# The first three q, k units of an attention kernel, made together by chunks of tokens

## The chip, the cores and the metric

The kernel runs on one core of one Trainium2 chip, in one launch. The metric is the device time of the kernel in microseconds, the median of the runs shown. The core has five engines with a queue of instructions each: TensorE (PE, with its weight loads shown apart as PEld), VectorE (DVE), ScalarE (ACT), GpSimd (POOL) and SyncE (SP, which here only issues DMAs). Engines wait for each other and for DMAs through semaphores.

## The reference

The layer is a sum of two branches on the same tokens, mixed by a gate of each token:

```python
x = A_x                                              # 1 x 2048 x 448
g = _sigmoid((x * gate_w).sum(-1, keepdims=True))
qkv = (x @ wqkv).reshape(B, S, 3, H, Dh)             # 16 heads of 28
p = softmax(q k^T * Dh ** -0.5);  a = (p v) @ wo
gate = x @ W_gate; gate = gate * (gate > 0)          # 448 x 1792
b = (gate * (x @ W_up)) @ W_down
return g * a + (1 - g) * b
```

All arrays are float32. The tokens are the same `x` in both branches.

## The kernel before, in words

Float32 operands are split into a high part (rounded to the format in which TensorE multiplies fast) and a low part, the remainder. `act_high` (line 130, ACT) makes the high part; `low` (line 136, DVE) or `pool_low` (line 139, POOL) subtracts it from the source. A product then has three terms: high by high, low by high, high by low. The 448 input features lie as four chunks of 128 partitions (the last is 64 features twice), so one output tile is the sum of the eleven matmuls of `TERMS`: a pair (a, b) takes part a of the weights `W` and part b of the tokens, and b % 4 is the chunk.

The first 100 us or so make q, k and v. Tokens come in four blocks of 512 (`tb`), weights in groups of 224 columns, which is 4 heads of k and q halves (`GD` = 112, two of it). A **unit** (tb, c), function `qk`, is 128 columns of q, k for one block of tokens: 11 matmuls (line 352) into one PSUM bank, then ACT copies the high part out, DVE makes the remainder (both into a tile `st` or half of the unused tile `K2`), and POOL issues a DMA (line 359) that stores both to `qk_d` in DRAM. A v unit (`vproj`, line 370) makes 128 tokens of v. The banks of units go round in a ring of four (0, 1, 5, 4); three `st` tiles and two halves of `K2` go round in a ring of five, and the sixth unit made waits for the store of the first.

Head h's K and Q are then fetched back from `qk_d` by SP (lines 175, 180, 182), four row blocks each and a block of zeros, and the first score matmul (line 191) reads all of K0 and Q0. The fetch of head 0 needs the units (0,0), (1,0), (2,0), (3,0) stored.

The order of work is written out by hand: each engine runs its queue in the order in which the code calls it. The first lines of the program are `load_w`, `load_x` (DMAs), `split_first` (the first weight group and the first tokens, by chunks), `split_w`, `split_x`, and calls of `qk`. Eleven matmuls on zeros ahead of the first unit (line 398, `WARM`) keep TensorE running until data come. The three staging tiles `xr` for tokens go round (`bufs=3`), the staging tile `wr` for weights is a single one, and the space of `V[:, 1]`, not needed until later, is used as a second one. POOL also fills rows of `K0`, `K1` (line 411) and columns of `V` (lines 406, 407) before its first store.

Of the kernel before, what the change touches and what calls it, by code (L numbers as in the profile page):

```python
# [18 lines left out]
P = 128  # L19
# [5 lines left out]
GD = G * DH  # L25
# [8 lines left out]
NQ = 2 * D // P  # L34

WC = 1408
WARM = 11

EARLY = (5, 5, 4, 4, 4, 3, 3, 3, 2, 2, 2, 2, 1, 1, 1, 1)

# [38 lines left out]
def gated_mix_kernel(ctx, tc, x, wq, wo, wgu, wd, out):  # L79
# [49 lines left out]
    def act_high(dst, src):  # L129
        nc.scalar.activation(dst, src, AF.Copy)  # L130
# [90 lines left out]
    def xf(tb, b):  # L221
        return X[tb][b // 4][:, b % 4]
# [13 lines left out]
    with tc.tile_pool(name="qkv", bufs=1) as pa:  # L236
        W = pa.tile([P, 7, WC], F32R, name="W")

        def load_w(c):
            c0, c1 = c * 2 * GD, (c + 1) * 2 * GD if c < G + 1 else 2 * D + VC  # L240

            if c in (0, 2, 5):
                wr = V[:, 1].rearrange("p k h d -> p (k h d)")[:, :4 * (2 * GD + 2)]
                wr = wr.rearrange("p (c n) -> p c n", c=4)
            else:
                wr = pa.tile([P, 4, 2 * GD + 2], F32, name=f"wr_{c0}", tag="wr", bufs=1)
            wr = wr[:, :, :c1 - c0]
            if c > 0:
                nc.sync.dma_start(wr, wq[:, :, c0:c1])
            return wr, c0, c1  # L250

        def split_w(wr, c0, c1):

            ways = [[(W[:, :, c0:c1], wr)]]
            if c0 < 2 * D:
                w, r = (ap.rearrange(f"p c {n} -> p c a j d", a=2, j=4)
                        for ap, n in ((W[:, :, c0:c1], "(j a d)"), (wr, "(a j d)")))
                ways = [[(w[:, :, a], r[:, :, a]) for a in range(2)]]

                if c0 == 2 * GD:  # L260
                    ways = [[(w[:, :, :, 0], r[:, :, :, 0])], [(w[:, :, a, 1:], r[:, :, a, 1:]) for a in range(2)]]
            for way in ways:
                for w, r in way:
                    act_high(w[:, 0:3], r[:, 0:3])
                    low(w[:, 3:6], r[:, 0:3], w[:, 0:3])
                for w, r in way:
                    act_high(w[:, 6], r[:, 3])
                    low(w[64:, 6], r[64:, 3], w[64:, 6])

        def split_first(wr, xr):  # L270

            r = wr.rearrange("p c (a j d) -> p c a j d", a=2, j=4)
            w = W[:, :, :2 * GD].rearrange("p c (j a d) -> p c a j d", a=2, j=4)

            def weights(c):
                act_high(w[:, c if c < 3 else 6], r[:, c])
                yield

                take = pool_low if c else low
                if c < 3:  # L280
                    take(w[:, 3 + c], r[:, c], w[:, c])
                else:
                    take(w[64:, 6], r[64:, 3], w[64:, 6])
                yield

            def tokens(c):
                part = xr[c // 2][2][:, c % 2:c % 2 + 1]
                act_high(X[0][0][:, c:c + 1], part)
                yield
                low(X[0][1][:, c:c + 1], part, X[0][0][:, c:c + 1])  # L290
                yield

            for group in ((weights(0), tokens(0)), (weights(1), tokens(1)), (weights(2), weights(3)),
                          (tokens(2), tokens(3))):
                for _ in range(2):
                    for part in group:
                        next(part)

        def load_x(tb):
            r = []  # L300
            for c in range(0, 4, 2):
                xr = pa.tile([P, 2, TB], F32, name=f"xr_{tb}_{c}", tag="stg", bufs=3)
                for a, b in ((c, c + 1), (c + 1, c + 2)) if tb == 0 else ((c, c + 2),):
                    nc.sync.dma_start(xr[:, a - c:b - c], x[:, a:b, tb * TB:(tb + 1) * TB])  # L304
                if tb + c == 0:
                    load_first(nc.sync, 2, 4)
                r.append((c, c + 2, xr))
            return r

# [39 lines left out]
        def qk(tb, c, terms=TERMS, among=()):  # L349
            ps = ps_any(c == NQ - 1)  # L350
            for n, (a, b) in enumerate(terms):
                nc.tensor.matmul(ps, W[:, a, c * P:(c + 1) * P], xf(tb, b), start=(n == 0), stop=(n == NT - 1))  # L352
                mix(n, among)
            st = st_tile(tb, c)

            def send():
# [21 lines left out]
                    nc.gpsimd.dma_start(v_d[g][:, k - 3:k + 1], V[:, g, k - 3:k + 1])  # L378


        w0 = load_w(0)

        def load_first(queue, a, b):
            queue.dma_start(w0[0][:, a:b], wq[:, a:b, w0[1]:w0[2]])  # L384
# [24 lines left out]
        split_first(w0[0], x0)  # L409
        for k in K[:2]:  # L410
            nc.gpsimd.memset(f32(k)[96:128], -1.0)
# [24 lines left out]
        w3 = load_w(3)  # L436
        load_k(0)
        load_q(0)

# [451 lines left out]
```

## Time and profile before

| | |
|---|---|
| median of 3 runs | 1259.94 us (1259.93 to 1260.57) |
| span of the profiled execution, first to last instruction | 1258.2 us |
| the median of the runs, less that span | 1.74 us |
| PE busy | 1252.8 us, 100% |
| DVE, ACT, POOL busy | 854.8, 748.4, 374.3 us |
| q, k and v matmuls by chunks of x (line 352) | 308, in 28 units of 11 |
| DMA share, 20 to 30 us | 1.04 and 1.02 by slices of 5 us |

A line of the timeline gives start, duration, engine, line, operation, output and inputs, shape, count, and in brackets the idle time ahead of it and what ended it. A line of the chain gives start, duration and what the end of the program hung on there. In tables by stage, columns are the stretch, its length, then busy time and count of PE, PEld, DVE, ACT and POOL, the granted share of TensorE's clock, the busy share of the DMA engines and GB/s. A DMA line gives the transfer, the queue, the count, its size, and the time from issue to landing where it is known. `q0` is the queue of POOL's DMAs, `q1` that of SP's, `q10` that of ACT's. A busy PE is not PE at its peak, since the ends of matmuls are modelled.

### The profile page before, as it was taken

To read this page: it belongs to the slowest core of one execution; us is meant where nothing else is said; L and a number is where in the kernel's file an instruction comes from. 1 tells how busy PE (TensorE), PEld (TensorE's weight loads), DVE (VectorE), ACT (ScalarE), POOL (GpSimd) and SP (SyncE) were. 2 spreads that over 40 slices of the span, in tenths; PEclk is the share of its full clock that TensorE was granted. 3 is DMA by queue.
4 is the path that set the end of the run, shared out by engine and by line. 5 is a ranking of instruction groups with operands and counts; after the bars stand their busy time and mean duration, and the time that the engine had idled before them with its cause. 6 is when DMAs were issued, how large, how long until landed. Compare 5 with 4: busy or idle time off the path is not lost.

```text
span 1258.2 us, 18270 instructions
## 1 busy us (share of the span) xinstructions
PE 1252.8 (100%) x6687; PEld 919.1 (73%) x6687; DVE 854.8 (68%) x1363; ACT 748.4 (59%) x1424; POOL 374.3 (30%) x569
## 2 busy tenths in 40 slices
PE   9999999999999999999999999999999999999998
PEld 6888866677666676666766667766667666899997
DVE  6599767687777797776977778877778224663342
ACT  6312767686666776666866667766677773312121
POOL 4222222312334123423133331134222444651020
PEclk9999999999999999999999999999999999999999
DMA  8955453144245314241544323142431226634432
GB/s 302 315 206 209 117 155 99 50 106 104 60 115 173 81 43 121 68 113 44 130 121 127 100 80 90 43 122 67 114 94 50 84 85 208 223 110 138 145 106 79
DMA packets 54113, 151.00 MB, mean 120 GB/s; under 512 B 10304, under 2 KB 17416, under 8 KB 49160
## 3 DMA queue, kind: packets, MB, share of 16 engines
q1 hardware_dynamic: 36632, 100.44, 29.2%
q0 software_dynamic: 16960, 48.94, 11.0%
q8 instruction: 52, 0.85, 0.3%
q10 hardware_dynamic: 432, 0.46, 0.1%
q14 instruction: 37, 0.30, 0.1%
HBM read 104.16 MB, written 46.03 MB: 119 GB/s over the span
## 4 chain that ended last, share of the span: by engine, by line
PE 99%; DMA 0%; SPq 0%; DVE 0%; ACT 0%; issue 0%
PE b L526 22%; PE b L191 19%; PE b L217 19%; PE b L560 18%; PE b L789 11%; PE b L352 5%; PE b L370 3%; PE b L744 3%; DMA xr<-x 0%; PE b L199 0%; SPq L304 0%; DVE X L136 0%; DVE y L795 0%; ACT X L130 0%; SPq L384 0%
## 5 line engine op out<-in xcount | busy, mean ns | idle before, releaser
L192 DVE TENSOR_REDUCE mx<-b 128x1 f32<-128x512 f32 x1024 | 646.5, 685 | 51.2 <-PE b L191 50.7
L219 ACT ACTIVATE P<-b 128x512 f32<-128x512 f32 x840 | 467.1, 599 | 160.8 <-PE b L217 139.0
L526 PE MATMUL b<-X,wg 128*128 128x512 f32 (+1 forms) x1232 | 415.3, 394 | 0.0
L191 PE MATMUL b<-K,Q 128*128 128x512 f32 x1024 | 389.6, 391 | 0.0
L217 PE MATMUL b<-Q,K 128*128 128x512 f32 x1024 | 389.3, 390 | 0.0
L526 PEld LDWEIGHTS b<-X,wg 128*128 128x128 f32 (+1 forms) x1232 | 220.2, 187 | 53.8 <-issue 9.3
L217 PEld LDWEIGHTS b<-Q,K 128*128 128x128 f32 x1024 | 192.3, 188 | 46.3 <-issue 6.7
L191 PEld LDWEIGHTS b<-K,Q 128*128 128x128 f32 x1024 | 192.4, 188 | 44.3 <-issue 5.9
L560 PE MATMUL b<-P,V 128*32 128x512 f32 x1680 | 188.2, 593 | 0.0
L548 POOL DMA_DIRECT2D h_d<-h x56 | 31.3, 558 | 405.4 <-DVE h L542 354.9
L139 POOL TENSOR_TENSOR wg<-wgr,wg 128x384 fp32r<-128x384 f32 x200 | 143.2, 731 | 10.4 <-DVE wg L133 2.0
L560 PEld LDWEIGHTS b<-P,V 128*32 128x32 f32 x1680 | 52.7, 110 | 120.0 <-issue 116.8
L789 PE MATMUL b<-WD,hh 128*128 128x448 f32 x672 | 138.5, 365 | 0.0
L219 ACT ACTIVATE V<-b 128x512 f32<-128x512 f32 x184 | 105.0, 599 | 48.8 <-PE b L217 42.3
L789 PEld LDWEIGHTS b<-WD,hh 128*128 128x128 f32 x672 | 126.2, 188 | 10.3
L130 ACT ACTIVATE hh<-hr 128x512 fp32r<-128x512 f32 x56 | 35.3, 631 | 124.7 <-PE b L789 120.2
L136 DVE TENSOR_TENSOR hh<-hr,hh 128x512 fp32r<-128x512 f32 x56 | 45.7, 815 | 66.4 <-ACT hh L130 66.3
L352 PE MATMUL b<-X,W 128*128 128x512 f32 x308 | 83.1, 393 | 0.1
L566 DVE TENSOR_TENSOR os<-b,os 128x512 f32<-128x512 f32 x16 | 11.1, 692 | 86.5 <-PE b L560 86.5
L352 PEld LDWEIGHTS b<-X,W 128*128 128x128 f32 x308 | 57.4, 188 | 14.5 <-DVE X L136 1.6
L130 ACT ACTIVATE wg<-wgr 128x384 fp32r<-128x384 f32 x156 | 62.2, 490 | 7.9 <-DMA wgr<-wgu 3.9
L575 POOL DMA_DIRECT2D l_d<-rs x16 | 8.9, 559 | 186.2 <-DVE rs L574 186.2
(74 smaller groups left out, 665.6 us busy)
## 6 DMA issues: line engine op xcount, KB each, us to landing
wgr<-wgu SPq DMA_DIRECT2D x55, 512.0 KB
K<-qk_d SPq DMA_DIRECT2D x64, 224.0 KB
Q<-qk_d SPq DMA_DIRECT2D x64, 224.0 KB
h_d<-h POOLq DMA_DIRECT2D x56, 256.0 KB, 2.7
hr<-h_d SPq DMA_DIRECT2D x56, 256.0 KB
qk_d<-st POOLq DMA_DIRECT2D x21, 512.0 KB, 4.2
x_d<-X POOLq DMA_DIRECT2D x6, 1024.0 KB, 5.4
X<-x_d SPq DMA_DIRECT2D x24, 256.0 KB
```

The lines of the kernel that those rows point to most:

```text
L130: nc.scalar.activation(dst, src, AF.Copy)
L136: nc.vector.tensor_tensor(dst, src, f32(high), op=OP.subtract)
L139: nc.gpsimd.tensor_tensor(dst, src, f32(high), op=OP.subtract)
L191: nc.tensor.matmul(ps, Q[h][:, u * P:(u + 1) * P], K[h % 3][:, c * TB:(c + 1) * TB], start=True, stop=True)
L192: nc.vector.tensor_reduce(MX[h][:, 4 * u + c:4 * u + c + 1], ps, axis=AX.X, op=OP.max)
L217: nc.tensor.matmul(ps, K[h % 3][:, kt * P:(kt + 1) * P], Q[h][:, j * TB:(j + 1) * TB], start=True, stop=True)
L219: nc.scalar.activation(PT[i][:, j], ps, AF.Exp, scale=SCALE)
L352: nc.tensor.matmul(ps, W[:, a, c * P:(c + 1) * P], xf(tb, b), start=(n == 0), stop=(n == NT - 1))
L370: nc.tensor.matmul(ps[:, :VC], xf(tb, b)[:, t * P:(t + 1) * P], W[:, a, 2 * D:2 * D + VC], start=(n == 0), stop=(n == NT - 1))
L526: nc.tensor.matmul(ps, WS[i][rows, s, a], xf(i // NF, b)[rows], start=(n == 0), stop=(n == NT - 1))
L560: nc.tensor.matmul(po[32 * j:32 * j + 32], V[:, h // 4 % 2, i % NK, h % 4], p[:, j], start=(i == i0), stop=(i == i0 + ni - 1))
L789: nc.tensor.matmul(ACC[i // NF][t][:, :D], HH[i][:, a, t * P:(t + 1) * P], WD[:, f, b], start=(f == 0 and n == 0), stop=(f == NF - 1 and n ...
```

## The change

Three units of the first token block, (0,0), (0,1) and (0,2), are made together in three banks, chunk by chunk (`qk_first`). For that the first two weight groups (448 columns) are needed with each chunk. They come in one staging space (`V[:, 1]`), each chunk's 224 or 448 columns right behind that chunk's tokens in SP's queue; only the first chunk's first 224 columns go by ACT's queue. ACT splits per chunk the tokens and both weight groups; DVE makes the remainder of the tokens and of the first group, POOL that of the second. In before, POOL made three remainders of the first group, and the second group came whole and was split on ACT and DVE after all tokens.

The units that follow are in another order: (1,0), (1,1), (1,2), (2,0), (2,1), (3,0), where it was (0,1), (1,0), (1,1), (0,2), (2,0), (2,1), (1,2), (3,0). Group 2's load uses the tile `wr`, not `V[:, 1]`, so that group 4's, in the same tile, is issued after group 2 is split. The split of group 4 is called ahead of unit (3,0), where it stood behind it. Eight warming passes stand where eleven stood.

```diff
-WARM = 11
+WARM = 8
...
-            if c in (0, 2, 5):
+            if c == 5:
                 wr = V[:, 1].rearrange("p k h d -> p (k h d)")[:, :4 * (2 * GD + 2)]
...
-            if c > 0:
-                nc.sync.dma_start(wr, wq[:, :, c0:c1])
+            nc.sync.dma_start(wr, wq[:, :, c0:c1])
...
-            def weights(c):
-                act_high(w[:, c if c < 3 else 6], r[:, c])
+            def weights(g, c):
+                r = wr[:, c, 2 * GD * g:2 * GD * (g + 1)].rearrange("p (a j d) -> p a j d", a=2, j=4)
+                w = W[:, :, 2 * GD * g:2 * GD * (g + 1)].rearrange("p c (j a d) -> p c a j d", a=2, j=4)
+                act_high(w[:, c if c < 3 else 6], r)
                 yield
 
-                take = pool_low if c else low
+                take = pool_low if g else low
...
-            for group in ((weights(0), tokens(0)), (weights(1), tokens(1)), (weights(2), weights(3)),
-                          (tokens(2), tokens(3))):
+            for c in range(4):
+                group = [weights(0, c), tokens(c), weights(1, c)]
+                if c:
+                    group = group[1:2] + group[:1] + group[2:]
                 for _ in range(2):
                     for part in group:
                         next(part)
...
                     nc.sync.dma_start(xr[:, a - c:b - c], x[:, a:b, tb * TB:(tb + 1) * TB])
-                if tb + c == 0:
-                    load_first(nc.sync, 2, 4)
+                    if tb == 0:
+                        load_first(nc.sync, a, a == 0, 2)
...
+        def qk_first():
+
+            units = [(c, ps_any()) for c in range(3)]
+            for c in range(4):
+                terms = [t for t in TERMS if t[1] % 4 == c]
+                order = [(t, u) for t in terms for u in units]
+                if c == 0:
+                    order = [(terms[n], units[k]) for n, k in ((0, 0), (1, 0), (0, 1), (0, 2), (2, 0), (2, 1), (2, 2), (1, 1), (1, 2))]
+                for (a, b), (u, ps) in order:
+                    nc.tensor.matmul(ps, W[:, a, u * P:(u + 1) * P], xf(0, b), start=b == 0 and a == 0,
+                                     stop=(a, b) == terms[-1] and c == 3)
+            for u, ps in units:
+                send_qk(0, u, ps)
...
-        w0 = load_w(0)
+        w0 = V[:, 1].rearrange("p k h d -> p (k h d)")[:, :4 * 4 * GD].rearrange("p (c n) -> p c n", c=4)
...
-        for c in range(2):
-            load_first(nc.scalar, c, c + 1)
+        load_first(nc.scalar, 0, 0, 1)
         x0 = load_x(0)
-        w1 = load_w(1)
         x1 = load_x(1)
...
-        split_w(*w1)
-        qk(0, 0, BY_CHUNK)
         split_x(1, x1)
+        qk_first()
...
-        qk(0, 1, HIGH_FIRST)
+        qk(1, 0)
         split_x(2, x2)
         x3 = load_x(3)
-        qk(1, 0)
+        qk(1, 1)
         split_w(*w2)
-        qk(1, 1)
-        qk(0, 2)
+        qk(1, 2)
         split_x(3, x3)
         w4 = load_w(4)
         qk(2, 0)
         w5 = load_w(5)
         qk(2, 1)
-        qk(1, 2)
-        qk(3, 0)
         split_w(*w4)
         w3 = load_w(3)
+        qk(3, 0)
         load_k(0)
```

TensorE's first matmuls behind the warming passes. `X0` are the high parts of the first tokens, `X1` their remainders, `b_0`, `b_1`, `b_4` are banks; in brackets stand the engines that a row waits for. Before, one unit alone:

```order
L352 MATMUL b_0_69<-X0_105,W_118 128x512 [waits Activation_49]
L352 MATMUL b_0_69<-X0_105,W_118 128x512 [waits DVE_49]
L352 MATMUL b_0_69<-X1_106,W_118 128x512 [waits DVE_49]
L352 MATMUL b_0_69<-X0_105,W_118 128x512 [waits Activation_49]
L352 MATMUL b_0_69<-X0_105,W_118 128x512 [waits Pool_49]
L352 MATMUL b_0_69<-X1_106,W_118 128x512 [waits DVE_49]
```

The same place in the changed kernel:

```order
L363 MATMUL b_0_69<-X0_105,W_118 128x512 [waits Activation_49]
L363 MATMUL b_0_69<-X0_105,W_118 128x512 [waits DVE_49]
L363 MATMUL b_1_70<-X0_105,W_118 128x512 [waits Activation_49]
L363 MATMUL b_4_73<-X0_105,W_118 128x512
L363 MATMUL b_0_69<-X1_106,W_118 128x512 [waits DVE_49]
L363 MATMUL b_1_70<-X1_106,W_118 128x512
L363 MATMUL b_4_73<-X1_106,W_118 128x512
L363 MATMUL b_1_70<-X0_105,W_118 128x512 [waits Pool_49]
L363 MATMUL b_4_73<-X0_105,W_118 128x512
```

The two units that came second and fifth have moved in between the terms of the first: one chunk now serves nine matmuls, not three.

ACT from the tokens of block 3 to the copy of unit (3,0). `xr_3_0` and `xr_3_2` are the halves of that block, `st_t_c` is the copy of unit (t,c), `wr_896` is weight group 4, `DMASW` is a store issued by POOL, `DMAHW` a load. The copy into `K2` behind `wr_896` in the changed kernel, and ahead of it before, is unit (3,0). Before:

```order
L130 ACTIVATE X0_3_119<-xr_3_0_241 128x1024 [waits DMAHW5_49]
L130 ACTIVATE X0_3_119<-xr_3_2_243 128x1024 [waits DMAHW6_49]
L130 ACTIVATE st_2_0_313<-b_1_70 128x512 [waits DMASW1_49,DVE_49,PE_49]
L130 ACTIVATE st_2_1_329<-b_4_73 128x512 [waits DMASW2_49,DVE_49,PE_49]
L130 ACTIVATE st_1_2_344<-b_5_74 128x512 [waits DMASW3_49,DVE_49,PE_49]
L130 ACTIVATE K2_114<-b_0_69 128x512 [waits DMASW4_49,DVE_49,PE_49]
L130 ACTIVATE W_118<-wr_896_300 128x3x224 [waits DMAHW7_49,Pool_49]
```

In the changed kernel:

```order
L130 ACTIVATE st_1_2_301<-b_1_70 128x512 [waits DMASW1_49,DVE_49,PE_49]
L130 ACTIVATE X0_3_119<-xr_3_0_264 128x1024 [waits DMAHW6_49]
L130 ACTIVATE X0_3_119<-xr_3_2_266 128x1024 [waits DMAHW7_49]
L130 ACTIVATE st_2_0_322<-b_4_73 128x512 [waits DMASW2_49,DVE_49,PE_49]
L130 ACTIVATE st_2_1_338<-b_5_74 128x512 [waits DMASW3_49,DVE_49,PE_49]
L130 ACTIVATE W_118<-wr_896_309 128x3x224 [waits DMAHW0_49,Pool_49]
L130 ACTIVATE W_118<-wr_896_309 128x224
L130 ACTIVATE K2_114<-b_0_69 128x512 [waits DMASW4_49,DVE_49,PE_49]
```

The copy that waits for the first store (`DMASW1`) stood behind block 3 and now stands ahead of it; the split of group 4 stood behind the copy of (3,0) and now stands ahead of it.

SP's queue from the tokens of block 2 on; `V` is the space that weights borrow. Before:

```order
L304 DMA xr_2_2_219<-x 128x2x512 [waits DMAHW0_49,DVE_49]
L249 DMA V_111<-wq 128x4x224 [waits DMAHW4_49,Pool_49]
L304 DMA xr_3_0_241<-x 128x2x512 [waits DMAHW1_49,DVE_49]
L304 DMA xr_3_2_243<-x 128x2x512 [waits DMAHW2_49,DVE_49]
L249 DMA wr_896_300<-wq 128x4x224 [waits DMAHW7_49]
L249 DMA V_111<-wq 128x4x226 [waits DMAHW4_49,DVE_49]
L249 DMA wr_672_366<-wq 128x4x224 [waits DMAHW7_49,DVE_49]
```

In the changed kernel:

```order
L302 DMA xr_2_2_242<-x 128x2x512 [waits DMAHW4_49,DMAHW1_49,DVE_49]
L248 DMA wr_448_244<-wq 128x4x224
L302 DMA xr_3_0_264<-x 128x2x512 [waits DMAHW6_49,DMAHW2_49,DVE_49]
L302 DMA xr_3_2_266<-x 128x2x512 [waits DMAHW3_49,DVE_49]
L248 DMA wr_896_309<-wq 128x4x224 [waits DMAHW5_49,DMAHW0_49,DVE_49]
L248 DMA V_111<-wq 128x4x226 [waits Pool_49]
L248 DMA wr_672_346<-wq 128x4x224 [waits DMAHW0_49,DVE_49]
```

The order of the transfers is the same; the wait for a split on DVE has moved from group 5 (`V`, 226 columns) to group 4 (`wr_896`), one place ahead.

More of the change, by code (lines that the diff above doesn't have):

```diff
@@ L258, in split_w @@
                 ways = [[(w[:, :, a], r[:, :, a]) for a in range(2)]]
-                if c0 == 2 * GD:
-                    ways = [[(w[:, :, :, 0], r[:, :, :, 0])], [(w[:, :, a, 1:], r[:, :, a, 1:]) for a in range(2)]]
             for way in ways:
@@ L378, in vproj, with load_first @@
                     nc.gpsimd.dma_start(v_d[g][:, k - 3:k + 1], V[:, g, k - 3:k + 1])
-        w0 = load_w(0)
-        def load_first(queue, a, b):
-            queue.dma_start(w0[0][:, a:b], wq[:, a:b, w0[1]:w0[2]])
-        for c in range(2):
-            load_first(nc.scalar, c, c + 1)
+        w0 = V[:, 1].rearrange("p k h d -> p (k h d)")[:, :4 * 4 * GD].rearrange("p (c n) -> p c n", c=4)
+        def load_first(queue, c, a, b):
+            queue.dma_start(w0[:, c, a * 2 * GD:b * 2 * GD], wq[:, c, a * 2 * GD:b * 2 * GD])
+        load_first(nc.scalar, 0, 0, 1)
         x0 = load_x(0)
-        w1 = load_w(1)
         x1 = load_x(1)
@@ L407, in sum_columns @@
             nc.gpsimd.memset(V[:, g, :, :, DH:DH + 1], 1.0)
-        split_first(w0[0], x0)
+        split_first(w0, x0)
         for k in K[:2]:
```

8 lines of the change are left out of this document (4 added, 4 removed).

## The prediction, made before the result was known

> **What bounds the kernel now.** I read the page first (span, busy table, chain), then the chain over the first 60 us, then TensorE's weight loads in the first 10 us, since a matmul that waits shows there.
>
> ```profile
> span 1258.2 us, 18270 instructions
> PE 1252.8 (100%) x6687; PEld 919.1 (73%) x6687; DVE 854.8 (68%) x1363; ACT 748.4 (59%) x1424; POOL 374.3 (30%) x569
> PE 99%; DMA 0%; SPq 0%; DVE 0%; ACT 0%; issue 0%
> ...
> 2.64 4.97 DMA xr<-x
> 7.63 0.64 ACT X L130
> 8.30 0.99 DVE X L136
> 9.33 30.44 PE b L352 x133
> 39.77 4.47 PE b L370 x22
> ```
>
> TensorE is the bound from 9.33 us to the end. Before that the chain runs through a transfer (the last chunk of the first tokens), its split on ACT and DVE, and only then into matmuls that never wait again. So the change can win only what lies ahead of 9.33, and can lose wherever a matmul behind it starts to wait. One matmul costs 30.44/133 = 0.229 us.
>
> ```profile
> 4.16 0.15 PEld L398 LDWEIGHTS <-V 128*128 128x128 bf16 x1 [0.28 <-issue]
> 4.49 0.31 PEld L398 LDWEIGHTS <-V 128*128 128x128 bf16 x2 [0.17 <-issue]
> 5.37 0.30 PEld L352 LDWEIGHTS b<-X,W 128*128 128x128 f32 x2 [0.57 <-ACT X L130]
> ...
> 9.33 0.30 PEld L352 LDWEIGHTS b<-X,W 128*128 128x128 f32 x2 [0.36 <-DVE X L136]
> ...
> 4.70 0.59 PE L398 MATMUL b<-V 128*128 128x512 bf16 x2
> ...
> 5.37:9.33 3.96, 3.89 (x10) 1.70 (x10) 3.06 (x5) 3.13 (x9) 3.12 (x4) 1.00 1.04 367
> ```
>
> The last two rows: the warming passes end at 4.70 + 0.59 = 5.29, and in the 3.96 us from the first real matmul (5.37) to 9.33 only 10 matmuls are issued; the "busy" 3.89 is modelled ends, not work. At 0.229 each they are worth 2.29 us.
>
> **Part 1, three units by chunks.** The first unit's eleven terms need all four chunks of tokens, so TensorE starves at their arrival. With three units open, each chunk carries 9, 9, 9 and 6 matmuls, 2.06 us of work or 1.37. The first can start where it does now, 5.37 (it needs the same chunk of tokens and weights). Chunk 1 is then wanted at 7.43, chunk 2 at 9.49, chunk 3 at 11.55. What stands against that:
>
> ```profile
> 5.70 0.61 ACT L130 ACTIVATE X<-xr 128x512 fp32r<-128x512 f32 x1
> 6.22 0.66 ACT L130 ACTIVATE W<-V 128x224 fp32r<-128x224 f32 x2
> 6.93 1.33 ACT L130 ACTIVATE X<-xr 128x512 fp32r<-128x512 f32 x2
> 8.94 1.42 ACT L130 ACTIVATE W<-wr 128x168 fp32r<-128x168 f32 x6 [0.67 <-DMA wr<-wq]
> ...
> 6.68 2.05 POOL L139 TENSOR_TENSOR W<-V,W 128x224 fp32r<-128x224 f32 x2 [0.19 <-ACT W L130]
> 8.79 3.56 POOL L411 MEMSET K<- 32x2048 f32 x2
> ```
>
> The bytes up to the end of the second weight group are the same (1024 KB of tokens, 896 of weights) and in before the last are landed by 8.94, when ACT stops waiting for them. Chunked, the last piece lands at about 8.9 again. ACT per chunk: one token split (about 0.6) and two weight splits (0.33 each), 1.3; DVE a token and a weight remainder, 1.1; POOL one remainder of about 1.0 (2.05/2). Chunk 1 is high by about 6.7 and its remainders by 7.6, chunk 2 by 8.2 and 9.2, chunk 3 by 9.5 and 10.5, each ahead of its matmuls by half a microsecond or more. So 33 matmuls run without a break from 5.37, and the stream stands 9.33 - 5.37 - 2.29 = 1.67 us ahead of before. That is the whole gain on offer. A row of before bounds it below: if chunk 3's pieces came 2 us later than reckoned, 1 us of it would go.
>
> **Part 2, eight warming passes.** The three removed ones end at 5.29, under the wait until 5.37 for the first token split: nothing won. If the tokens landed sooner, they would be in the way by at most 0.6. The loads of the passes come every 0.43 us up to 4.16 and then two within 0.31: the slow clock ends near 4.4, and eight passes (the ninth starts at about 4.49) just reach that point. Taken as nothing; rival 3 takes it otherwise.
>
> **Part 3, what is late next.** Three things move with the reordering, on ACT, POOL and SP. (a) POOL gets one more remainder, and its fills of K start behind chunk 3: about 10.4, not 8.79. The first store of q, k waits behind the fills.
>
> ```profile
> 14.01 0.78 POOL L359 DMA_DIRECT2D qk_d<-st  x1
> 29.16 2.17 POOL L359 DMA_DIRECT2D qk_d<-st  x3 [5.58 <-DVE st L136]
> 31.45 0.72 POOL L359 DMA_DIRECT2D qk_d<-K  x1
> ...
> qk_d<-st POOLq DMA_DIRECT2D x1, 512.0 KB, 8.2
> ...
> qk_d<-st POOLq DMA_DIRECT2D x3, 512.0 KB, 4.4
> qk_d<-K POOLq DMA_DIRECT2D x1, 512.0 KB, 6.7
> ...
> 23.11 1.06 ACT L130 ACTIVATE X<-xr 128x1024 fp32r<-128x1024 f32 x1 [2.03 <-DMA xr<-x]
> 25.94 1.06 ACT L130 ACTIVATE X<-xr 128x1024 fp32r<-128x1024 f32 x1 [1.78 <-DMA xr<-x]
> ```
>
> The first store goes from 14.01 to about 15.6, and with its 8.2 us lands at 23.8 (with the 4.4 of later stores, at 20.0). On ACT the copy of unit (1,2) reuses that store's buffer, and the splits of token block 3 now stand behind it. Unit (3,0) is the ninth unit as before; it starts after 88 matmuls, at 5.37 + 20.15 = 25.5, and wants the third chunk at 26.4. With the copy at 23.8 the two splits (about 1.0 apart) end at 25.4 and 26.4, if the second half lands by 25.4, against 25.94 now. The second half meets more stores on the way but has a later first store; I take no stall here, with 0 to 1.2 as bounds.
>
> (b) Weight group 4 now takes the one buffer that group 2 leaves, so its load is issued at about 21.5 (before, at 16.4), still behind the tokens of block 3 in SP's queue, which end only at 25.9. So I leave its landing where it is, 30.7. But its split now stands **ahead** of the copy of (3,0) on ACT and DVE:
>
> ```profile
> 29.83 0.60 ACT L130 ACTIVATE K<-b 128x512 fp32r<-128x512 f32 x1 [1.37 <-PE b L352]
> 30.73 1.05 ACT L130 ACTIVATE W<-wr 128x672 fp32r<-128x672 f32 x2 [0.30 <-DMA wr<-wq]
> ...
> 31.52 1.28 DVE L136 TENSOR_TENSOR W<-wr,W 128x672 fp32r<-128x672 f32 x2 [0.37 <-ACT W L130]
> 34.16 0.69 DVE L136 TENSOR_TENSOR K<-b,K 128x512 fp32r<-128x512 f32 x1
> ...
> 38.15 2.43 SPq L175 DMA_DIRECT2D K<-qk_d  x4
> 53.11 0.38 SPq L180 DMA_DIRECT2D Q<-qk_d  x1
> ...
> 54.04 0.19 PEld L191 LDWEIGHTS b<-K,Q 128*128 128x128 f32 x1
> ```
>
> In before the copy comes at 29.83, its store goes at 31.45 and lands 6.7 later, at 38.15, and in that instant SP begins to fetch the first head's K and Q. The first score matmul reads them at 54.04. SP's issue at 53.11 waits for the semaphore that the last of these fetches carried, so they are complete by 53.1: the slack is 0.94 us, less than the 1.67 to be won. This is the term that cuts the gain. In the new order: group 4 lands 30.7, remainders end 31.52 + 1.28 = 32.8, copy's remainder 33.5, store 33.5 instead of 31.45. It lands 4.4 to 6.7 later. I take 4.4, because the three stores just ahead of it, issued from 29.16 on before, now go some 1 to 4 us earlier while it goes 2 later, so it queues less: 37.9. The fetch takes 53.1 - 38.15 = 14.95: complete at 52.85. TensorE would be there at 54.04 - 1.67 = 52.37, waits 0.48, and keeps 54.04 - 52.85 = 1.19. With 6.7 the fetch ends at 55.15 and 1.1 us is lost.
>
> (c) The first v unit, at 39.77 - 1.67 = 38.1, wants the bank of (3,1), whose remainder stands behind group 5's on DVE and ended at 34.85. Cover 3.2 us, so nothing.
>
> The sum: 1.67 - 0.48 = 1.19 us off the span of 1258.2, which becomes 1257.0. The median of the three runs shown is 1259.94, 1.74 above that span; the same distance gives 1258.75, call it **1258.8**.
>
> **A rule weighed.** The row is 26.5 to 29 us, when stores and weights share the DMA engines:
>
> ```profile
> q0 software_dynamic: 220, 0.82, 80.4%
> q1 hardware_dynamic: 226, 0.19, 22.6%
> ```
>
> In these 2.5 us SP's queue moved 0.19 MB, 76 KB/us, in as many packets as the stores' 0.82 MB. The Trainium skill, "DMA: Bandwidth & Descriptors", section "Queues, rings and completion order", has each engine take turns between queues by the packet, not by the byte. By that rule, and the trace agrees, the weights' short rows lose whenever stores are queued. Going by it the 448 KB of group 4 would need 5.9 us from 25.9 on and land at 31.8; the sum would be 0.1 us of gain. It speaks against the change, and is priced next.
>
> **The rivals.**
> 1. Group 4 lands late and holds the store of (3,0): slower. From its landing L the first fetch is complete at L + 2.8 + 4.4 + 14.95 = L + 22.1, against the 54.04 at which TensorE read it before, so from L = 31.9 the kernel is slower. For it: before, a gap in the stores (5.58 us of POOL's idleness ahead of 29.16) let the weights through; three early stores may close it. At 76 KB/us L is 31.8, and group 5 (452 KB more) lands at 37.7, which stalls the v unit by 2.7 and makes the kernel 1.0 slower. With L = 33.7 it is 1.8 slower, and with 6.7 for the store 4.1. Against it: group 4 has the same things ahead of it as before. Time 1259.9 to 1264, most likely 1261.
> 2. The splits of token block 3 hold TensorE at 25.5, through the first store's late landing. A landing of 25 us stalls 1.1, one at 26 more than eats the gain. Some of it is cover for the wait at 52.4. Time 1259.3 to 1260.2.
> 3. The clock gate opens later, since eight passes fill only 3.3 us. If it opened as long again after 4.4, at 7.7, the 2.33 us from 5.37 would hold 5.4 matmuls of 0.43 where 10.2 were reckoned: 1.1 us late, a gain of 0.57, time 1259.4; if twice as long, at 11.0, it is 2.6 late and 0.96 slower, 1260.9. Before cannot show this loss, as its TensorE starves there anyway. Against: the rows above have it open by 4.49. The Trainium skill, "TensorE: Matmul & The Clock Gate", section "What's actually happening", says that the window which decides this runs free of the kernel's start; its table "Why this matters for your kernels" asks for 4 us of passes or more. No run here shows another phase.
>
> **How the numbers follow.** Chances: forecast 0.57, rival 1 0.26, rival 2 0.09, rival 3 0.08. A fifth of a per cent, about what a measurement of this kernel can tell from no change, is 2.5 us: 1257.4 to 1262.5. The most to be won is 1.67, so a faster verdict needs an earlier first matmul too: 0.02. Slower needs rival 1 with both of its prices, 0.08. The rest, 0.90, is no change. The range: below, the whole head start, 1258.3, less the runs' scatter, 1258.1; above, rival 1 without its tail, 1261.6.
>
> **What would show it.** Right: matmuls of the first units about 0.23 apart from 5.4 on, the first v unit near 38.1, the first score matmul's load at 52.4 to 53.2, with a wait for the fetches ahead of it, everything behind shifted by the same amount. Wrong: a wait for ACT's splits near 25.5, group 4 landed after 32, SP's first fetch of K after 38.2, or real matmuls 0.43 apart.

## The result, and the profile after

The changed kernel takes **1261.73 us** (median of 21 runs, 1260.11 to 1263.67), the kernel before on the same chip 1260.21 (21 runs, 1259.68 to 1260.58). The ratio is 1.0013, with a 95% interval of 1.0007 to 1.0019: slower by 0.13%, where 1.2 us of gain was forecast. The time lies just outside the predicted range (to 1261.6), and within the 0.2% that was called no change. The runs also scatter over 3.6 us, where before they stay within 0.9.

The first stretch, the chain of work of the changed kernel (start, duration, what the end hung on there), then TensorE's matmuls and weight loads in the same profile:

```profile
5.34 10.15 PE b L363 x33
15.50 2.51 PE b L350 x11
...
19.61 1.24 DVE X L136
20.86 6.92 DMA xr<-x
27.80 1.07 ACT X L130
28.92 11.98 PE b L350 x51
40.90 4.47 PE b L385 x22
```
```profile
1.20 3.59 PE L411 MATMUL b<-V 128*128 128x512 bf16 x8 [1.20 <-DVE V L407]
5.34 10.15 PE L363 MATMUL b<-X,W 128*128 128x512 f32 x33 [0.56 <-ACT X L130]
```
```profile
28.91 0.99 PEld L350 LDWEIGHTS b<-X,W 128*128 128x128 f32 x5 [0.47 <-ACT X L130]
30.18 1.91 PEld L350 LDWEIGHTS b<-X,W 128*128 128x128 f32 x9 [0.27 <-DVE X L136]
```

The change did what it says: the 33 matmuls of the three first units run from 5.34 without a gap, where before ten stood between 5.37 and 9.33. But they take 10.15 us, where 33 by 0.229 are 7.56. The profile's table by stage shows why:

```profile
5.34:10.40 5.06, 5.06 (x12) 4.04 (x13) 4.26 (x7) 3.96 (x10) 3.05 (x4) 1.00 1.03 373
10.40:15.50 5.10, 5.10 (x24) 4.20 (x23) 2.43 (x3) 2.64 (x4) 4.87 (x8) 1.00 0.69 215
```

Twelve matmuls go in the first 5.06 us, one each 0.42, and 24 in the next 5.10, one each 0.21. The trace's record of the clock has its first entry, full speed, at 10.40 us (in the kernel before at 4.37); the column of the granted clock says 1.00 in the first row only because nothing is recorded ahead of that entry.

The second place is block 3 of the tokens. Its second half lands at 27.78, its split on ACT comes at 27.80, and TensorE's third chunk of unit (3,0) waits for it until 28.91. Before, the same split came at 25.94. The load is issued late; SP's queue, the two halves of block 3, before and after:

```profile
14.28 2.10 SPq L304 DMA_DIRECT2D xr<-x  x2
```
```profile
13.99 7.24 SPq L302 DMA_DIRECT2D xr<-x  x2
```

Before, the second of the two goes at 16.01, in the changed kernel at 20.86. It waits for a staging tile, which DVE's remainder of block 2's first half gives free (19.61 + 1.24 in the chain above); that split now stands behind the copy of unit (1,0) on ACT and DVE, and (1,0) comes only after three units. And it meets other traffic. POOL's stores, of 512 KB each, in the changed kernel:

```profile
16.71 2.25 POOL L374 DMA_DIRECT2D qk_d<-st  x3 [0.68 <-DVE st L136]
19.65 0.73 POOL L374 DMA_DIRECT2D qk_d<-K  x1 [0.69 <-DVE K L136]
22.87 0.73 POOL L374 DMA_DIRECT2D qk_d<-K  x1 [2.49 <-DVE K L136]
```

Before, two went by 15.9 and the next at 20.09.

The sum by these rows: 33 matmuls from 5.34 would end at 12.90. In three of the kernels below the 110 matmuls that follow, up to the first v unit, run unbroken in 24.93 us. So the v unit would start at 37.83, against 39.77 before. The slow clock adds 15.50 - 12.90 = 2.60 and the wait 0.47, which makes 40.90, where it is. That is 1.13 late, and the first score product is as late (its result is reduced at 55.83, 54.70 before). The span is 1.7 longer; the other 0.6 comes near 1073 us, where TensorE's weight loads wait 0.75 us for a remainder of gate and up weights. The kernel with eleven passes below waits 0.48 there, five others 0.17 to 0.36, the kernel before not at all. It was not followed up.

### The profile page after: what moved, and what is told of

Same layout as the page of the kernel before. It is cut to its first block, busy times and chain, and to the rows that moved or that the text cites. A ratio compares the mean times of both kernels' runs of the same rounds, so it can differ in the third digit from the quotient of the medians.

```text
span 1259.9 us, 18260 instructions
## 1 busy us (share of the span) xinstructions
PE 1253.8 (100%) x6684; PEld 920.5 (73%) x6684; DVE 854.8 (68%) x1360; ACT 748.7 (59%) x1422; POOL 376.1 (30%) x570
## 4 chain that ended last, share of the span: by engine, by line
PE 98%; DMA 1%; DVE 0%; ACT 0%; issue 0%; DVEq 0%
PE b L536 22%; PE b L191 19%; PE b L217 19%; PE b L570 18%; PE b L799 11%; PE b L350 4%; PE b L385 3%; PE b L754 3%; PE b L363 1%; DMA xr<-x 1%; DMA V<-wq 0%; PE b L199 0%; ACT X L130 0%; DVE wg L136 0%; DVE X L136 0%; DVE y L805 0%
## 5 line engine op out<-in xcount | busy, mean ns | idle before, releaser
L799 PEld LDWEIGHTS b<-WD,hh 128*128 128x128 f32 x672 | 126.1, 188 | 10.4 <-DVE hh L136 0.2
L350 PE MATMUL b<-X,W 128*128 128x512 f32 x275 | 74.3, 391 | 0.0
L574 DVE COPY os<-b 128x512 f32<-128x512 f32 x16 | 11.1, 691 | 77.2 <-PE b L570 77.2
```

The source lines that it names most:

```text
L799: nc.tensor.matmul(ACC[i // NF][t][:, :D], HH[i][:, a, t * P:(t + 1) * P], WD[:, f, b], start=(f == 0 and n == 0), stop=(f == NF - 1 and n ...
```

## Experiments

All kernels are the changed one with the edit shown, unless said otherwise. Kernels of one group ran on one chip beside the kernel before (medians there 1260.18, 1260.24, 1260.14, 1260.17). The table gathers the profiled executions; its numbers are from the traces, the last column is the median of eleven runs (21 for the first row). "Clock" is when full speed is first granted, "tokens" the issue and the landing of the second half of block 3, "wait" TensorE's wait for it (weight loads), "score" how much later than in the kernel before DVE starts on the first score product (54.70 there).

| kernel | clock | 33 matmuls | tokens | wait | score | median, us |
|---|---|---|---|---|---|---|
| changed, first profile | 10.40 | 10.15 | 20.86, 27.78 | 0.47 | +1.13 | 1261.73 |
| changed, second profile | 5.22 | 7.88 | 18.48, 28.02 | 3.09 | +2.79 | 1262.27 |
| eleven passes | 4.35 | 7.78 | 18.32, 27.92 | 3.14 | +1.58 | 1261.80 |
| block 2 split earlier | 10.22 | 10.04 | 18.83, 28.49 | 1.24 | +1.82 | 1261.17 |
| one store put off, eleven | 5.68 | 7.93 | 18.80, 27.57 | 2.31 | +2.40 | 1260.46 |
| two stores put off, eleven | 3.90 | 7.83 | 18.25, 24.72 | 0 | -0.99 | 1259.17 |
| two stores put off | 5.98 | 8.12 | 18.7, 23.76 | 0 | -1.51 | 1258.95 |

### The clock: eleven passes after, eight before

The first theory was rival 3: the clock opens late and costs what the head start brings. Against it stood rival 2, the tokens of block 3.

```diff
-WARM = 8
+WARM = 11
```

> The changed kernel with eleven warming passes again, nothing else. Gate theory (in the profile of the changed kernel matmuls stay 0.43 us apart until 10.4 us; eight passes end at 4.6 and leave a gap until 5.34 that keeps the clock low): the passes last until 5.3 or longer, the clock is full by 4.4 to 7.7 us, the scatter of the runs shrinks from 3.6 us to about 1 us and the median falls by 1.3 us or more below the changed kernel's, to 1259.2 to 1260.4. Block-3 theory (the late tokens of block 3 hold TensorE near 28 us whatever the first units do): the stall grows to what the head start wins, median 1261 to 1262, no faster than the changed kernel.

Measured: 1261.80 us (1260.52 to 1263.61), ratio to before 1.0010 [1.0001, 1.0019]: neither faster nor steadier. Chain and weight loads:

```profile
1.20 4.08 PE b L411 x11
5.28 7.68 PE b L363 x33
12.96 2.51 PE b L350 x11
...
18.32 9.60 DMA xr<-x
27.95 1.06 ACT X L130
```
```profile
29.05 0.99 PEld L350 LDWEIGHTS b<-X,W 128*128 128x128 f32 x5 [3.14 <-ACT X L130]
...
55.75 0.19 PEld L191 LDWEIGHTS b<-K,Q 128*128 128x128 f32 x1 [0.51 <-issue]
```

With the clock open, the head start is there as forecast: 33 matmuls in 7.7 us, done at 12.96. All of it is then lost in one wait of 3.14 us, for the same tokens, which land at 27.92 although they were issued 2.5 us sooner. So the clock's 2.60 us in the first profile was no loss of its own: it was cover for a wait that would have stood there otherwise. As the sole cause, rival 3 falls.

The same part alone, in the kernel before:

```diff
-WARM = 11
+WARM = 8
```

> The kernel before with eight warming passes, nothing else. Gate theory: the gap behind the passes is the same, so the clock is late in most runs, but ahead of 9.3 us TensorE waits for data anyway; only the matmuls from 9.3 us to the opening (up to about 11) are slower, 0 to 1 us, plus the first ten at 0.43 (9.6 instead of 9.3): median 0.3 to 1.5 us above before, scatter 1.5 us or more. Block-3 theory: the passes lie under the wait for data, the time is that of before within 0.2 us and the scatter too.

Measured: 1260.10 (1259.80 to 1260.66), ratio 0.9997 [0.9988, 1.0006]. The clock opened at 7.05, and TensorE's part of the chain began at 8.67 (9.33 before), the first v unit at 39.73 (39.77): there the slow matmuls lie under the wait for tokens.

### Earlier splits

If the half waits for its staging tile, freeing the tile earlier should help: the split of block 2 goes ahead of unit (1,0), so that this unit's copy on ACT no longer stands in front of it.

```diff
-        qk(1, 0)
         split_x(2, x2)
+        qk(1, 0)
```

> The changed kernel with the splits of token block 2 called ahead of unit (1,0), so that on ACT and DVE they no longer stand behind that unit's copy, and SP's load of the second half of block 3, which waits for the staging tile they free, is issued at about 17 us and not at 20.9. Block-3 theory: that half lands by about 25 and not at 27.8, the wait near 28.5 us is gone, 0.2 to 2 us faster than the changed kernel in its slow runs, scatter smaller. Gate theory alone: the clock still opens late; the median falls by no more than the 0.2 us that the profile shows as a wait at 28.5, 1261.4 to 1261.8, scatter 3 us or more.

Measured: 1261.17 (1260.35 to 1264.09), ratio 1.0008 [0.9999, 1.0017]. The half is issued at 18.83, 2 us sooner, and lands at 28.49, later than in the first profile. With eleven passes as well:

> Both: eleven passes and the splits of block 2 ahead of (1,0). If the two causes are all there is, the whole head start of 1.67 us is kept where the clock opens early: median 1258.5 to 1259.5, faster than before. If the first head's fetch of K and Q (slack 0.94 us before) holds TensorE, the gain stops at about 1.0 us or less, with a wait at the first score matmul near 53 us.

Measured: 1261.62 (1260.00 to 1263.57), ratio 1.0008 [1.0000, 1.0017]. Here it lands by 26.2 and TensorE waits 0.97 us, but then 1.77 us at the first score product for the fetch of K and Q: group 4's split ran at 32.99, ahead of the copy of (3,0), whose store went at 36.09 and the fetch at 40.48. That is the forecast's term 3(b), larger than its 0.48.

The half is issued at 17.39, 18.32, 18.83 and 20.86 in these four and lands at 26.2, 27.9, 28.5 and 27.8. An earlier issue helps by less than it is earlier, or not at all, since the load then takes longer (8.8, 9.6, 9.7 and 6.9 us); before, from 16.01, it took 9.9.

### Staging the half early

The next edit takes the wait for a staging tile away altogether: the half lies in a free part of `V[:, 1]`, and SP issues its load at 14.4 to 15.

```diff
+                if (tb, c) == (NB - 1, 2):
+                    xr = V[:, 1].rearrange("p k h d -> p (k h d)")[:, 2 * TB:].rearrange("p (c t) -> p c t", c=2)
```

With eight and eleven passes, and both again with unit (3,0) called ahead of group 4's split:

> The changed kernel, except that the raw tokens of the second half of block 3 are staged in a part of V[:, 1] that is free then, so that SP issues their load right behind the first half's (about 14 us, not 20.9) and no longer waits for a staging tile. Theory 'the transfer' (the 0.99 to 3.1 us wait of TensorE near 26 to 29 is the second half of block 3, which comes late because its load queues behind the bunched stores): it lands at 21 to 24, TensorE does not wait there; the clock still opens near 10.3, which leaves the stream about 1 us behind the head start; the next wait is the first fetch of K and Q, 0 to 0.5. Time 1259.5 to 1261. Rival 'the stores' (any load behind about 16 us starves until the stores drain, whenever it is issued): lands at 26 or later, TensorE still waits 1 us or more near 26 to 29, 1261.5.

> The same with eleven warming passes. Theory 'the transfer': the clock opens near 4.4, 33 matmuls run unbroken from about 5.3, no wait near 26, TensorE reaches the first score product about 1.7 us earlier than in the kernel before and waits there 0.5 to 1.8 us for the fetch of K and Q (the split of group 4 stands ahead of the copy of unit (3,0)). Time 1259 to 1260.5. Rival 'the stores': the wait near 26 stays at 2 to 3 us, time 1261.5 to 1262.

> As the first of these, with the split of group 4 and the load of group 5's first buffer moved back behind the unit (3,0), so that this unit's store goes ahead. Theory 'the transfer': store of (3,0) at 31 to 32, SP's first fetch of K at 37 to 38.2, no wait at the first score product; but the clock opens near 10.3. Unit (4,0) may wait for group 4's split, up to 1 us. Time 1259.5 to 1260.5. Rival 'the stores': the wait near 26 to 29 stays, 1261.5.

> Both, with eleven warming passes: every wait that has been seen is taken away. Theory: head start of 1.67 us kept but for 0 to 0.7, time 1258.5 to 1259.5, faster than both kernels by 0.05 to 0.15 per cent. Rival 'the stores': 1261 to 1262.

Measured, in that order: 1261.02 (1260.04 to 1263.58), ratio 1.0007 [0.9998, 1.0016]; 1262.76 (1260.73 to 1265.72), 1.0018 [1.0009, 1.0027]; 1260.46 (1259.46 to 1261.11), 0.9999 [0.9990, 1.0008]; 1260.44 (1258.65 to 1262.93), 1.0001 [0.9992, 1.0010]. The half, issued at 14.4 to 15.0, is split on ACT from 24.4 to 25.4. Only in the second kernel did ACT wait for it: there it lands at 25.4, after 10.4 us, later than the 21 to 24 expected; in the others it had landed by the time of its split. That suffices: the wait near 26 to 29 is gone in all four, and yet the second kernel is the slowest of all, and the fourth, which was to be 1 us faster than before, is level with it. In the second kernel's profile TensorE waits 1.05 us at the first v unit and 1.19 at the scores; but that run took 1260.85, and what its slower runs lost, up to 1265.72, no profile shows. The weight loads and the chain of the fourth:

```profile
PEld b L388 <- DVE K L136: 2.3, 1, 2.3
```
```profile
22.12 14.93 DMA V<-wq
...
37.08 0.78 ACT W L130
...
39.20 0.70 DVE K L136
...
39.95 4.75 PE b L388 x22
```

What is loaded late next, weight group 5, is issued at 22.12 and takes 14.93 us; the split of it holds a remainder on DVE, and that holds the bank that the first v unit wants: 2.3 us. Between 22 and 37 us the stores moved 4.12 MB, SP's queue 1.11. Before a wait can be cured for good, then, one must ask what makes every load of SP's queue late in this stretch. (With eight passes the two kernels of this group opened the clock at 9.89 and 10.31, lost 2.3 to 2.6 us by it, and the first met a wait of 0.7 at the scores.)

### Putting two stores off

The suspect was the bunch of stores: three units finish together, POOL issues 1.5 MB at 15.5 to 17, and only a third of it, unit (0,0), is wanted by the first head's fetch. In this edit the other two stay in halves of `V[:, 2]` and `V[:, 3]` that v units write only later, and are stored behind the first head's fetches, near 47 us; the second head's fetch stands behind them, and the fills of those columns of `V` come later. Nothing is left out.

```diff
             k = sent[0]
             sent[0] += 1
+            if (tb, c) in ((0, 1), (0, 2)):
+                return V[:, c + 1, :NK // 2] ... .bitcast(F32R)
...
-                nc.gpsimd.dma_start(qk_d[...], f32(st))
+                later.append(store) if (tb, c) in ((0, 1), (0, 2)) else store()
...
-            if n == 6:
+            if n == 7:
+                for store in later:
+                    store()
                 load_k(1)
```

With eight passes, and with eleven:

> The changed kernel with two stores put off: q, k of the units (0,1) and (0,2) stay in free halves of V[:, 2] and V[:, 3] and are stored (1 MB) only after the first head's fetches are issued, near 50 us; the fetch of the second head's K and Q stands behind them. Nothing is left out. Theory 'bytes' (the loads of SP's queue come late because the stores of the first units share the DMA engines with them): the second half of block 3 lands at 23 to 25.5, not 27.8, TensorE's wait near 28 is 0 to 0.3 (0.99 before), group 4 lands at 28 to 30 and group 5 earlier than 33.5. The clock still opens near 10. Time 1260.0 to 1260.8. Rival 'latency' (the load is late by its own size or by when it was issued): lands at 27 or later, 1261.5.

> The same with eleven warming passes, to be read against the changed kernel with eleven, in which that half was issued at 18.32, took 9.6 us and held TensorE for 3.11. Theory 'bytes': it takes 5 to 7 us, the wait is 0 to 0.8; the first fetch of K and Q is the next to bind. Time 1259.3 to 1260.5. Rival 'latency': 9 us or more, 1261.8.

Measured: **1258.95** (1258.39 to 1260.33), ratio to before 0.9993 [0.9984, 1.0002], and 1259.17 (1258.55 to 1261.68), 0.9993 [0.9984, 1.0002]. The kernel with eight passes is 2.8 us below the changed kernel's median, the kernel before being 1260.1 and 1260.2 beside them. Against the kernel before, the gain of about 1 us is not clear of noise in either: both intervals just include 1. With eight passes the clock, expected near 10, opened at 5.98 in the profile, so what a late one would cost here was not seen. The chain of that kernel:

```profile
5.20 8.12 PE b L365 x33
13.32 24.93 PE b L352 x110
38.26 4.47 PE b L390 x22
```

Nothing holds TensorE between 5.20 and the scores. The DMA queues during the load of the half say what changed; first eleven passes as they were (18.32 to 27.95 us), then with two stores put off (18.25 to 24.72); packets, MB, share of 16 engines:

```profile
q0 software_dynamic: 711, 2.59, 71.2%
q1 hardware_dynamic: 673, 0.93, 31.1%
```
```profile
q0 software_dynamic: 421, 1.54, 58.7%
q1 hardware_dynamic: 531, 0.93, 41.1%
```

SP's queue (q1) moved the same 0.93 MB in both. Beside it went 2.59 MB of stores in one case and 1.54 in the other. The total is 3.54 MB in 9.63 us and 2.49 in 6.47, or 368 and 385 KB/us: the engines are full (the two shares add up to 102 and 100%), and the half lands when the stores that share them have gone through. Issued at the same 18.3, it comes 3.2 us sooner, for 1.05 MB less. (Before, between 16.01 and 25.94, the stores moved 1.57 MB, but SP's queue 1.83, 344 KB/us in all; so the half took 9.9 us there as well, and landed in time because it was issued early.) In the first case the two queues moved nearly as many packets, 711 and 673, but 3.6 KB each against 1.4. The rule that the prediction weighed, turns by packet and not by byte (the Trainium skill, "DMA: Bandwidth & Descriptors", section "Queues, rings and completion order"), agrees with this row.

With eleven passes the fetch is next to bind, in the chain and the weight loads:

```profile
41.05 11.01 DMA Q<-qk_d
```
```profile
53.18 0.19 PEld L191 LDWEIGHTS b<-K,Q 128*128 128x128 f32 x1 [1.08 <-issue]
```

This is the world of the forecast: the head start whole up to the v unit, then a wait at the first score, and 0.99 us kept of it.

### Three controls

Is the put-off a gain by itself? The same edit in the kernel before:

> The kernel before with the same two stores put off. Theory: before has no wait of TensorE between 9.33 and the first head's scores, so earlier loads win nothing there, and the gain of 1.2 us that the changed kernel has with the put-off is its own head start: 1260.1, within 0.3 of the kernel before, matmuls unbroken from about 9.3. Rival (the put-off is a gain by itself, whatever the first units do): 1259 to 1259.3.

Measured: 1260.17 (1259.78 to 1260.77) against 1260.17, ratio 1.0000 [0.9991, 1.0009]. Its stream begins at 9.19 and runs as before, in the chain:

```profile
9.19 30.44 PE b L354 x133
```

So the put-off is no gain by itself: what the changed kernel wins with it, 1.51 us at the scores with eight passes, is its own head start, and the put-off only lets it through.

Does the delay follow the bytes? One store put off, that of (0,2), eleven passes:

> The changed kernel with eleven warming passes and one store put off, that of (0,2), 512 KB. Theory 'bytes': the second half of block 3 lands between the two others, 25 to 27 (27.95 with none put off, 24.75 with two), TensorE's wait 0.3 to 2, and the first fetch waits 0.5 to 1 behind it; 1259.8 to 1261. Rival (a threshold, or the buffer that the put-off frees): lands as with none or as with two.

Measured: 1260.46 (1258.95 to 1262.88), ratio 1.0002 [0.9993, 1.0011]: the median lies between none and two put off (1261.80, 1259.17). But in its profile the half lands at 27.57, outside the 25 to 27 expected, close to none put off, and TensorE waits 2.31. That profiled run took 1262.73, the second slowest of the eleven. Its DMA queues from issue to landing (18.80 to 27.57 us):

```profile
q0 software_dynamic: 574, 2.10, 61.4%
q1 hardware_dynamic: 800, 1.12, 39.6%
```

The stores moved half a MB less than with none put off, but SP's queue 0.19 MB more, and the total went at 368 KB/us again (3.23 MB in 8.77 us). That agrees with engines that are full all the time; why SP's queue had more to move was not followed up. The median speaks for the bytes, the one profile does not tell them from a threshold.

And the changed kernel once more, for another phase of the clock:

> The changed kernel as it is, beside the two. Where its clock opens by 7 us in the profile, the wait for block 3 is over 2 us; where it opens near 10, it is below 1: the two delays cover each other, and the first v unit starts near 40.9 either way. 1261.7.

Measured: 1262.27 (1260.96 to 1262.65), ratio 1.0013 [1.0004, 1.0022]. The clock opened at 5.22 this time, with eight passes, and the wait was over 2 us as expected; but the v unit came at 42.55, not near 40.9. TensorE's matmuls, and the table by stage around the wait:

```profile
5.24 7.88 PE L363 MATMUL b<-X,W 128*128 128x512 f32 x33 [0.45 <-ACT X L130]
12.96 13.54 PE L350 MATMUL b<-X,W 128*128 128x512 f32 x59
29.16 13.40 PE L350 MATMUL b<-X,W 128*128 128x512 f32 x51 [2.66 <-ACT X L130]
```
```profile
25.00:29.11 4.11, 1.49 (x7) 0.91 (x5) 1.01 (x1) 1.06 (x2) 0.55 (x1) 1.00 1.03 318
29.11:32.52 3.41, 3.37 (x8) 2.69 (x9) 2.42 (x3) 0.96 (x2) 1.26 (x2) 0.50 0.74 272
32.52:36.00 3.48, 3.48 (x16) 2.90 (x16) 2.52 (x4) 3.07 (x6) 0.46 (x2) 1.00 0.82 308
```

The clock closed. Right behind the wait it was granted at 0.50 for 3.41 us, eight matmuls went where sixteen go, and 3.41/2 = 1.7 us were lost on top of the wait. Wait and closing make 4.5 us of this profile: the 110 matmuls end at 42.55 instead of 13.12 + 24.93 = 38.05. Of the 21 runs of the changed kernel, the ten at 1262.05 us and above are those with a mean clock of 0.998 or 0.999 over the whole run, the eleven below have 1.000. That the clock closed behind this wait was seen in this profile and in that of the one store put off (29.57 to 32.99, 0.50); for the others it is argued only. A mean of 0.999 alone does not show it: the kernel before has it in some of its runs, and the profile with two stores put off and eight passes (1258.39 us, 0.999) closes only at 1255.26, at the end of the program.

### A version that beats both

Early staging, (3,0) ahead of group 4's split, and the two stores put off, with eleven and with eight passes:

> Put-off stores, block 3's second half staged early, group 4's split behind unit (3,0), eleven warming passes. Theory 'bytes': group 5 lands before 34 (37.08 without the put-off), no wait at the first v unit (1.9 without), SP's first fetch of K at 36 to 37, the first score product at 53 to 53.5, 1.2 to 1.67 us ahead of the kernel before, kept to the end: 1258.5 to 1259. Rival: the fetch (some 3.7 MB in 15 us) is bound by itself, and the score products start no earlier than 0.5 us ahead: 1259.7.

> The same with eight passes: what the clock's late opening costs when nothing else binds. If it opens near 10.3, 2.3 to 2.6 us behind the kernel with eleven at the first v unit: 1260.5 to 1261. If by 7, about 1: 1259.5.

Measured: **1258.82** (1257.96 to 1259.79), ratio to before 0.9989 [0.9980, 0.9998], and **1258.58** (1258.01 to 1260.02), 0.9988 [0.9979, 0.9996]. Both are faster than the kernel before by about 0.1%, with intervals that exclude 1, and their medians lie some 3 us below that of the changed one (on another chip). No wait of TensorE is left up to the scores, SP's first fetch of K goes at 35.1 and 35.3 (39.66 in the changed kernel), and the first score product stands 0.77 and 1.33 us ahead of before. The kernel with eleven passes is not better: in its profile the passes end at 6.06 and the first real matmul starts there, 0.8 later than with eight, since the clock opened only at 7.04. That price of eleven was not foreseen; that the kernel with eight would stand behind by a late clock did not come about in its profile, where it opened at 6.29.

## Why the prediction was wrong

**Part 1** (a head start of 1.67 us, 33 matmuls unbroken from 5.37) was right where the clock was open: 7.68 us from 5.28 in the chain of the kernel with eleven passes, done at 12.96. The arrival of chunks, the splits and POOL's share were reckoned well enough to leave no gap.

**Part 2** (eight passes "taken as nothing") failed. They end at 4.79, and the first real matmul comes 0.55 later. Of eight profiles with eight passes, four opened the clock at 9.89 to 10.40 and four at 5.22 to 7.05; of the nine with eleven, none later than 7.04. Rival 3 had the size: open at 11.0, 2.6 late; measured 10.40 and 2.60. Its chance of 0.08 was much too low. The kernel before opened at 4.37 in one profile, and that was read as a property of the passes, not of the moment. The Trainium skill, "TensorE: Matmul & The Clock Gate", table "Why this matters for your kernels", asks for 4 us of passes; the eight last 3.6, and in four of these eight profiles that was too short.

**Part 3(a)** ("I take no stall here, with 0 to 1.2 as bounds") is the step that decided. Measured: 0.47 us where the clock was late, 3.1 where it was not. It worked out when ACT would be free to split the half (25.4) and left the landing as a condition ("if the second half lands by 25.4, against 25.94 now"); it landed at 27.8 to 28.0. Two things were left out. The issue waits for the staging tile that block 2 gives free, and moved from 16.01 to between 18.3 and 20.9, with the copy of (1,0) now ahead of that block's split; the prediction followed the splits of block 3 and not those of block 2. And "the second half meets more stores on the way but has a later first store" weighed the two as equal; where the clock was open it met 2.54 MB (second profile; 2.59 with eleven passes), where 1.57 went before. In the first profile it met 1.74 MB in 6.9 us, but was issued at 20.86. Neither alone makes the wait: with the early issue it is gone though all stores are there, and with two stores fewer it is gone though the issue stays at 18.3 to 18.7. It takes both, the late issue and the bunch of stores. Against the kernel before, the load itself is no slower (9.5 and 9.6 us with the clock open, 9.9 before, when more of SP's own loads went beside it): what is later is its issue, and the stores use up what SP's shorter queue would have given back. The prediction had the rate for this (76 KB/us for SP's queue while stores are queued) and spent it on group 4 alone, not on the transfer that came first. Rival 2 named the place, but through a copy that waits on ACT for the first store, and ended at 1260.2.

Not reckoned at all was that such a wait can close the clock behind it, 1.7 us more, as two profiles show; that this lifts the tail to 1263.7 is argued, since no run above 1262.73 was profiled. And the two failed steps are not a sum: a late clock hides the wait, an open one makes it, and mending the clock alone moved the median by 0.1, staging the half early by 0.7.

**Part 3(b)** was right in kind. In the changed kernel it does not bind, as TensorE is late by itself; SP's first fetch of K goes at 39.66, later than the 37.9 reckoned, since group 4's split came at 31.30 and the store at 34.41. In five of the other profiles it showed, at 0.5 to 1.8 us (0.48 forecast). **Part 3(c)**, no stall at the v unit, holds in the changed kernel and failed with early staging, at 2.3 us. **Rival 1** (group 4 lands late) gave 1261 as its likeliest time, near the result, but another mechanism made it: group 4 was split at 31.30 and 32.62 in the two profiles, on both sides of the 31.9 from which it was to lose, and no wait came of it, TensorE being later still.

## What to carry to other kernels

A head start is worth nothing where a transfer behind it comes later than the earlier work wants it. Work that is made together also stores together: list the bytes of all queues between the change and the next place where data are awaited, divide by the rate of full engines (about 370 KB/us here), and put off the stores that nobody reads soon. And follow each load back to what frees its buffer: a split that moves behind a copy delays the issue of a load one block on. Where two delays meet at one place, mending one only uncovers the other; and count a wait of 2 to 3 us on TensorE at more than its length, since the clock may close behind it.

## What the runs showed that was not expected

- TensorE's clock closed for one stretch of 3.41 us (0.50 granted) behind waits of 3.1 and 2.3 us (weight loads), though seven to ten matmuls start in the 4.1 us ahead of the closing. Behind the wait of 3.1 us with eleven passes it did not close; counted in stretches of 3.41 from the opening at 4.35, that wait is cut at 28.24, 2.3 us before and 0.8 behind. Counted in the same way from 5.68, the wait of 2.3 us with one store put off lies whole in the stretch that ends at 29.57, where the clock closed. So 2.3 us of one stretch closed it in one profile and not in the other, and where the limit lies is not settled. The Trainium skill, "TensorE: Matmul & The Clock Gate", table "Why this matters for your kernels", warns of gaps above some 3 us; a gap of 2.3 us sufficed in one profile here.
- The moment of opening moves over some 3 us with the same passes (3.90 to 7.04 with eleven), and misses by a whole stretch more with eight. The kernel before hides this under its own wait for tokens: with eight passes its median of eleven runs is the same, though its one profile opened at 7.05 and not late.
- Loading a 512 KB half took 9.6 us beside 2.59 MB of stores and 6.5 beside 1.54; a load of 452 KB took 14.9.
